# Two of three weights loaded and cast by GpSimd's queue, with a new order of all operations: sliding-window attention feeding an RWKV channel mix

## The chip, the core and the metric

The kernel runs on one core of a Trainium2 chip. The metric is the device time of one execution in microseconds; smaller is better. Before the change it is 167.43 us, the median of two runs (167.19 and 167.66). One further execution was profiled.

## What is computed

Attention over 4 batches, 8 heads, 768 positions and a head size of 64, with a window of 128 keys and 4 sink keys that every query sees. Its output, as rows of 512 features, goes into a channel mix with three weight matrices.

```python
scores = scale * np.matmul(q, k.transpose(0, 1, 3, 2))
keep = is_sink | in_window               # 4 sinks, window of 128
a = softmax(np.where(keep, scores, -1e9))
x = (a @ v) as [B, S, 512]
xk = mu_k * x + (1.0 - mu_k) * x_prev    # x_prev: x one position earlier
xr = mu_r * x + (1.0 - mu_r) * x_prev
k = np.maximum(xk @ w_k, 0.0)            # w_k 512 x 1024
v = k * k @ w_v                          # w_v 1024 x 512
r = 1.0 / (1.0 + np.exp(-(xr @ w_r)))    # w_r 512 x 512
return r * v
```

All inputs and the output are fp32; the matrix products run in bf16.

## The kernel before

**Units.** The work is cut into 12 units of 256 positions, numbered u = 0 to 11, three to a batch. For each unit the program records four groups of operations, which the functions of the same name make: `prepare` (cast q and k to bf16, transpose them on TensorE, copy the result out of PSUM, cast v), `attend` (scores, exponential, mask, product with v, division), `mix` (transpose x, form xk and xr on VectorE) and `ffn` (w_k product, ReLU and square, w_r product and tanh, w_v product, store). Units 0 and 1 get their mask as a matrix product added in PSUM (line 714), so that VectorE needn't multiply it in.

**Loads.** q, k, v and the weights come from HBM on SyncE's (SP's) queue. One unit's q or k is 512 KB and its v is two loads of 256 KB. For unit 0 the loads of q and k are halved by heads. The weights come as fp32 pieces of 1 MB (w_k in two, w_v in two, w_r in one) into three staging buffers named w32 (line 427). Ten casts then turn them into the bf16 tiles `wk_sb`, `wr_sb` and `wv_h` (lines 572 to 582): four for w_k, two for w_r and four for w_v, each of 128 x 1024 elements. On which engine each of them runs is in the table CHOICE. In the page, `wk_sb L564` on DVE and POOL and L558 on ACT are these casts.

**Order.** Nothing about the order is left to chance. The table ORDER lists for each engine (PE is TensorE, DVE VectorE, ACT ScalarE, POOL GpSimd, SP SyncE) the numbers of its operations in the order in which it issues them, and an engine that waits for one holds up all that stand behind it. A number is an operation's place in the program. `Plan.schedule` replays these lists with a cost for each operation. It does so to choose the buffer that each operation gets, and to see where TensorE would be idle: there it puts matrix products with a tile of zeros, called fills, whose result nothing reads (line 985, made in lines 264 to 275). They are there up to 32 us of planned time. How many stand at a place is fixed when the program is built. Line 241 doubles the planned cost of TensorE's operations up to 5.6 us, for a clock that isn't yet full.

**The first unit** of `ffn` can start once unit 0's xk is made (line 858) and w_k is in bf16. In the lists before the change TensorE's first w_k product, operation 206, stands behind the exponential of two head pairs of unit 1. The operations that the prediction follows there are, for units 0 and 1, the casts of line 596 (k, q) and line 644 (v), the copies out of PSUM of line 630, the exponentials of line 743 and, on POOL, the copy of the sink keys of line 661 (`ksink`).

Of the kernel before, what the change touches and what calls it, by code (L numbers as in the profile page):

```python
# [18 lines left out]
    82: "POOL", 83: "ACT", 89: "ACT", 97: "DVE", 99: "DVE", 100: "DVE", 103: "DVE", 104:  # L19
    "ACT", 137: "DVE", 140: "DVE", 141: "ACT", 143: "DVE", 150: "DVE", 178: "DVE", 181:  # L20
    "DVE", 183: "DVE", 187: "DVE", 190: "DVE", 191: "DVE", 193: "DVE", 200: "DVE", 209:
    "ACT", 213: "ACT", 217: "ACT", 258: "DVE", 270: "ACT", 271: "ACT", 276: "DVE", 292:
    "ACT", 339: "DVE", 344: "POOL", 346: "DVE", 349: "ACT", 350: "DVE", 352: "DVE", 359:
    "DVE", 367: "DVE", 372: "ACT", 376: "ACT", 380: "ACT", 419: "POOL", 421: "DVE", 422:
    "POOL", 428: "ACT", 430: "DVE", 437: "DVE", 446: "ACT", 450: "ACT", 454: "ACT", 458:
    "ACT", 497: "DVE", 499: "DVE", 500: "DVE", 505: "ACT", 527: "ACT", 535: "ACT", 576:
    "DVE", 579: "DVE", 584: "DVE", 585: "DVE", 594: "DVE", 603: "ACT", 607: "ACT", 615:
    "ACT", 654: "DVE", 660: "ACT", 661: "ACT", 663: "DVE", 679: "ACT", 683: "ACT", 691:
    "ACT", 728: "DVE", 732: "DVE", 734: "DVE", 736: "DVE", 742: "DVE", 749: "DVE", 758:
    "ACT", 762: "ACT", 766: "ACT", 770: "ACT", 807: "DVE", 811: "DVE", 813: "DVE", 814:  # L30
    "ACT", 823: "DVE", 832: "ACT", 836: "ACT", 883: "POOL", 887: "DVE", 889: "ACT", 890:
    "DVE", 892: "DVE", 899: "DVE", 907: "DVE", 908: "ACT", 916: "ACT", 920: "ACT", 958:
    "DVE", 965: "DVE", 978: "ACT", 982: "ACT", 986: "ACT", 1002: "ACT", 1013: "DVE",
# [24 lines left out]
        95, 92, 79, 108, 109, 101, 98, 118, 106, 119, 111, 115, 121, 125, 142, 132, 129,  # L58
        158, 138, 159, 149, 182, 156, 188, 135, 168, 169, 165, 234, 161, 175, 206, 171,
        207, 192, 210, 199, 211, 218, 214, 179, 215, 219, 185, 236, 297, 301, 289, 302,  # L60
        290, 298, 293, 247, 294, 239, 244, 224, 222, 250, 305, 275, 226, 255, 230, 227,
        262, 231, 282, 307, 259, 313, 268, 317, 309, 265, 310, 314, 342, 328, 365, 369,
        366, 373, 347, 374, 370, 325, 320, 395, 331, 336, 381, 351, 377, 358, 378, 383,
        406, 393, 385, 273, 420, 386, 443, 451, 444, 389, 452, 425, 390, 398, 403, 409,
        473, 414, 455, 447, 429, 448, 436, 456, 484, 471, 461, 459, 467, 498, 468, 524,
        528, 525, 529, 476, 503, 492, 552, 536, 481, 537, 487, 463, 508, 464, 517, 532,
        510, 563, 555, 533, 542, 560, 540, 577, 548, 586, 549, 600, 582, 604, 601, 605,
        566, 571, 630, 608, 612, 593, 609, 613, 616, 628, 641, 618, 544, 633, 545, 676,
        638, 677, 688, 680, 689, 681, 644, 649, 706, 662, 694, 684, 669, 620, 704, 717,
        685, 621, 692, 624, 755, 625, 756, 709, 714, 759, 720, 760, 763, 741, 764, 700,  # L70
        725, 696, 701, 739, 783, 697, 748, 767, 771, 768, 773, 786, 791, 794, 779, 775,
        780, 829, 776, 830, 837, 802, 815, 838, 833, 847, 834, 797, 845, 841, 822, 842,
        857, 859, 849, 853, 909, 905, 870, 906, 854, 850, 910, 862, 867, 917, 923, 918,
        913, 878, 891, 914, 935, 873, 921, 929, 898, 925, 933, 946, 930, 926, 971, 979,
        972, 975, 980, 976, 938, 943, 987, 949, 954, 983, 957, 984, 989, 995, 964, 991,
        996, 992, 999, 1003, 1000, 1004, 1011, 1007, 1012, 1017, 1008, 1019, 1015, 1020,
        1027, 1023, 1028, 1024,
    ),
    "DVE": (
        69, 70, 97, 100, 103, 99, 107, 80, 112, 113, 116, 117, 122, 123, 137, 126, 143,  # L80
        144, 127, 145, 181, 187, 146, 183, 140, 147, 150, 151, 148, 153, 154, 155, 152,
        81, 166, 162, 176, 163, 167, 177, 172, 173, 193, 84, 200, 194, 178, 195, 201, 196,
        202, 203, 197, 205, 198, 86, 221, 190, 238, 243, 191, 85, 204, 240, 245, 241, 249,
        246, 87, 88, 254, 276, 300, 251, 90, 256, 252, 296, 304, 257, 277, 228, 258, 232,
        278, 280, 284, 281, 339, 285, 287, 279, 288, 311, 286, 324, 346, 319, 315, 367,
        335, 330, 368, 321, 322, 326, 332, 327, 337, 333, 338, 352, 353, 359, 354, 360,
        355, 361, 362, 356, 397, 274, 421, 402, 363, 408, 357, 350, 387, 413, 399, 391,
        400, 410, 404, 405, 415, 411, 416, 364, 430, 500, 431, 437, 432, 434, 475, 438,
        497, 439, 433, 440, 491, 499, 469, 480, 486, 477, 435, 493, 478, 441, 494, 442,
        531, 482, 488, 483, 489, 509, 554, 465, 539, 559, 556, 579, 576, 512, 557, 519,  # L90
        513, 561, 562, 521, 514, 520, 515, 565, 550, 654, 570, 588, 516, 567, 572, 568,
        573, 523, 522, 594, 589, 595, 632, 584, 597, 585, 590, 637, 596, 634, 611, 635,
        591, 546, 639, 598, 640, 643, 648, 592, 599, 645, 650, 651, 663, 646, 728, 664,
        736, 665, 708, 713, 671, 672, 666, 622, 673, 667, 732, 719, 734, 626, 710, 715,
        711, 716, 724, 675, 742, 687, 721, 743, 668, 744, 726, 722, 727, 674, 702, 746,
        740, 807, 749, 790, 785, 698, 750, 811, 747, 787, 754, 745, 752, 792, 788, 751,
        793, 753, 801, 781, 777, 803, 804, 796, 817, 818, 798, 799, 819, 820, 840, 823,
        824, 826, 827, 825, 844, 887, 828, 861, 813, 866, 907, 855, 821, 851, 877, 863,
        868, 864, 869, 912, 872, 879, 892, 880, 893, 874, 875, 896, 894, 895, 899, 890,
        900, 901, 902, 942, 937, 931, 897, 927, 903, 948, 904, 953, 939, 940, 944, 945,  # L100
        974, 955, 950, 951, 958, 959, 956, 962, 960, 965, 961, 966, 967, 968, 997, 993,
        969, 970, 963, 1006, 1013, 1014, 1010, 1021, 1029, 1025,
    ),
    "ACT": (
        68, 67, 94, 91, 96, 93, 110, 114, 102, 104, 120, 124, 131, 128, 133, 130, 134,
        139, 160, 164, 157, 136, 141, 189, 174, 235, 170, 208, 83, 209, 212, 184, 180,
        216, 220, 186, 237, 242, 291, 299, 213, 303, 248, 295, 253, 223, 225, 217, 306,
# [28 lines left out]
class Plan:  # L136
# [28 lines left out]
    def schedule(self):  # L165
# [42 lines left out]
        while any(lines.values()):  # L208
            best = None
            for engine, line in lines.items():  # L210
                if not line or left[line[0]]:
                    continue
                i = line[0]
# [27 lines left out]
            if o["engine"] == "PE" and t < 5600.0:  # L241
                cost += min(cost, 5600.0 - t)
# [59 lines left out]
def kernel(  # L302
# [64 lines left out]
    def act(n):  # L367
        return 67.0 + 0.833 * n
# [669 lines left out]
```

## Time and profile before

| | us |
|---|---|
| median of the runs | 167.43 |
| time of the profiled execution | 168.37 |
| its span, first to last instruction | 166.7 |
| TensorE busy | 159.5 |
| TensorE's weight loads busy | 105.2 |
| VectorE busy | 145.6 |
| ScalarE busy | 133.6 |
| GpSimd busy | 16.3 |

The granted TensorE clock is 1.000 in the summary of the core. The span is the stretch that the profile shows; the profiled execution took 1.67 us more than it. Some rows of the page that the change touches, with the mean duration of one instruction: copies out of PSUM on ACT (line 630) 753 ns x13 and 752 ns x7, on DVE 731 ns x3 and 735 ns x1; weight casts on DVE 677 to 694 ns, on ACT 1049 and 1188 ns, on POOL 1112 ns; fp32 casts of 128 x 512 on ACT 618 to 659 ns, on DVE about 422 ns; fills (line 985) 594 ns x14.

A busy TensorE in the page isn't TensorE at its peak, since products are pipelined and their ends are modelled. The DMA line counts packets that overlap, so a stretch can show more than one full share.

### The profile page before, as it was taken

Reading aid. Unit: us, or ns where it says so; the run is one execution under the profiler, and the core shown is the slowest. Engines: PE = TensorE matmul, PEld = TensorE weight load, DVE = VectorE, ACT = ScalarE, POOL = GpSimd, SP = SyncE. Lnnn points to the kernel's source line nnn. Section 1 sums busy time; section 2 is a strip of 40 time slices with the busy share of each in tenths; the row PEclk is TensorE's granted clock in tenths of the full one; section 3 lists DMA queues with packets and bytes.
Section 4 is the critical chain, followed back from the end, with each engine's and each line's share of the span. In section 5 each row is a group of like instructions: output and inputs, shape, how many; then the busy total and the mean of one; then the engine's idle time right before and its main releaser. Section 6 shows DMA issues by size and latency. Waiting matters only on the chain.

```text
span 166.7 us, 4208 instructions
## 1 busy us (share of the span) xinstructions
PE 159.5 (96%) x1611; PEld 105.2 (63%) x1611; DVE 145.6 (87%) x378; ACT 133.6 (80%) x221; POOL 16.3 (10%) x43
## 2 busy tenths in 40 slices
PE   7999889999999999999999999999999999999991
PEld 2455567865577568486585775856575675684760
DVE  5249999999999999999999899899979988999832
ACT  3679959998999999998999999719779588754340
POOL 7800020000221201210000000210010000000000
PEclk9999999999999999999999999999999999999999
DMA  4999999999969979999996898779959782100403
GB/s 134 251 290 247 374 349 265 333 339 273 232 135 255 257 149 201 242 287 228 184 263 114 186 260 236 159 137 225 278 106 241 185 220 99 63 4 0 189 0 126
DMA packets 81762, 33.81 MB, mean 203 GB/s; under 512 B 63688, under 2 KB 76240, under 8 KB 81744
## 3 DMA queue, kind: packets, MB, share of 16 engines
q1 hardware_dynamic: 81728, 33.56, 84.7%
q8 instruction: 12, 0.20, 0.5%
q14 instruction: 6, 0.05, 0.1%
q10 hardware_dynamic: 16, 0.00, 0.0%
HBM read 24.12 MB, written 6.29 MB: 182 GB/s over the span
## 4 chain that ended last, share of the span: by engine, by line
PE 82%; DVE 8%; ACT 4%; DMA 2%; issue 2%; DVEq 0%; ACTq 0%
PE bank L908 24%; PE bank L965 22%; PE bank L947 12%; PE sc L707 6%; PE bank L781 6%; PE bank L820 3%; PE bank L622 3%; PE bank L769 2%; DMA qs<-in_q_dram 2%; ACT e L743 1%; PE bank L985 1%; PE sc L714 1%; DVE x L797 1%; PE bank L878 1%; DVE xk L858 1%
## 5 line engine op out<-in xcount | busy, mean ns | idle before, releaser
L908 PE MATMUL bank<-xk,wk_sb 128*128 128x256 bf16 x384 | 50.8, 273 | 0.8 <-DVE wk_sb L564 0.7
L743 ACT ACTIVATE e<-sc 128x1024 bf16<-128x1024 f32 (+1 forms) x48 | 45.5, 975 | 6.1 <-PE sc L707 6.0
L965 PE MATMUL bank<-wv_h,kk 128*128 128x512 bf16 x184 | 45.7, 380 | 0.0
L908 PEld LDWEIGHTS <-wk_sb 128*128 128x128 bf16 x384 | 35.5, 98 | 9.6 <-DVE wk_sb L564 1.2
L918 ACT ACTIVATE rl<-bank 128x512 bf16<-128x512 f32 x45 | 26.4, 609 | 13.9 <-PE bank L908 12.3
L965 PEld LDWEIGHTS <-kk 128*128 128x128 bf16 x184 | 16.8, 98 | 15.8 <-issue 0.5
L757 DVE TENSOR_TENSOR e<-e,mask 128x1024 bf16<-128x1024 bf16 (+1 forms) x40 | 25.2, 645 | 0.4 <-ACT e L743 0.2
L947 PE MATMUL bank<-wr_sb,xr 128*128 128x512 bf16 x96 | 24.3, 379 | 0.0
L858 DVE SCALAR_TENSOR_TENSOR xk<-td,mu_all,xt 128x256 bf16<-128x256 bf16 x48 | 22.8, 497 | 0.2
L858 DVE SCALAR_TENSOR_TENSOR xr<-td,mu_all,xt 128x256 bf16<-128x256 bf16 x48 | 22.6, 483 | 0.0
L935 ACT ACTIVATE kk<-rl 128x512 bf16<-128x512 bf16 x32 | 20.5, 646 | 0.1
L797 DVE TENSOR_TENSOR x<-bank,rec 128x256 bf16<-128x256 f32 x48 | 19.2, 415 | 0.5
L781 PE MATMUL bank<-vb,e 128*128 128x65 bf16 x352 | 18.7, 193 | 0.4 <-ACT e L743 0.3
L974 DVE SCALAR_TENSOR_TENSOR ob<-th,bank 128x512 f32<-128x512 f32 x23 | 15.6, 681 | 3.1 <-PE bank L965 2.7
L781 PEld LDWEIGHTS <-e 128*128 128x128 bf16 x352 | 16.3, 97 | 3.1 <-ACT e L743 0.9
L953 ACT ACTIVATE th<-bank 128x512 f32<-128x512 f32 x24 | 14.6, 618 | 1.9 <-PE bank L947 1.9
L707 PE MATMUL sc<-qt,kt 64*128 64x128 bf16 (+1 forms) x256 | 14.2, 242 | 0.3 <-ACT kt L630 0.3
L947 PEld LDWEIGHTS <-xr 128*128 128x128 bf16 x96 | 8.7, 98 | 7.0
L769 PE MATMUL bank<-vsink,es 128*128 128x130 bf16 x64 | 12.4, 221 | 0.1
L707 PEld LDWEIGHTS <-kt 64*128 64x128 bf16 x256 | 9.0, 95 | 5.4 <-issue 2.3
L630 ACT COPY qt<-bank 128x512 bf16<-128x512 bf16 x13 | 9.8, 753 | 1.6 <-PE bank L622 1.6
L847 DVE TENSOR_TENSOR td<-xt 128x512 bf16<-128x512 bf16 x24 | 10.6, 440 | 0.2
(75 smaller groups left out, 167.6 us busy)
## 6 DMA issues: line engine op xcount, KB each, us to landing
vs<-in_v_dram SPq DMA_DIRECT2D x24, 256.0 KB, 5.0
out_dram<-ob SPq DMA_DIRECT2D x23, 256.0 KB, 4.3
ks<-in_k_dram SPq DMA_DIRECT2D x18, 256.0 KB, 5.2
qs<-in_q_dram SPq DMA_DIRECT2D x7, 512.0 KB, 6.2
qs<-in_q_dram SPq DMA_DIRECT2D x10, 256.0 KB, 4.5
w<-in_moe_w_k_dram SPq DMA_DIRECT2D x2, 1024.0 KB, 8.3
w<-in_moe_w_v_dram SPq DMA_DIRECT2D x2, 1024.0 KB, 8.8
ks<-in_k_dram SPq DMA_DIRECT2D x3, 512.0 KB, 10.0
```

The lines of the kernel that those rows point to most:

```text
L707: nc.tensor.matmul(out=sc[:, a, o0:o1], lhsT=lhs[rows], rhs=rhs[rows], start=u not in BIAS, stop=True, skip_group_check=u in BIAS)
L743: nc.scalar.activation(out=buf[ek][:, :, lo:], in_=buf[sck][:, :, lo:], func=AF.Exp, scale=scale)
L757: nc.vector.tensor_tensor(out=at, in0=at, in1=m, op=ALU.mult)
L769: nc.tensor.matmul(out=o[:, g, :, :], lhsT=buf["es", u][:, 128 * g:128 * g + 128], rhs=vsink[b % 2][:, 2 * c:2 * c + 2, :], start=True, st ...
L781: nc.tensor.matmul(out=o[:, g, a, :], lhsT=e[:, a, e0:e0 + 128], rhs=rhs, start=(T == 0 and i == 0), stop=(i == len(blocks) - 1), skip_gro ...
L797: P.op("DVE", dve(256), lambda ok=ok, rk=rk, c=c: nc.vector.tensor_tensor(out=buf["x", u][:, :, 128 * c:128 * c + 128].rearrange("p g (a d ...
L858: nc.vector.scalar_tensor_tensor(out=buf[key][:, c0 + i, :], in0=buf[tk][:, i, :], scalar=mu[w][:, c0 + i:c0 + i + 1], in1=xt[:, c0 + i, t ...
L908: nc.tensor.matmul(out=ps[:, i, :], lhsT=wk_sb[:, c, 128 * f:128 * f + 128], rhs=xk[:, c, :], start=(c == 0), stop=(c == NC - 1), skip_gro ...
L918: nc.scalar.activation(out=buf[rk], in_=buf[psk].rearrange("p (i t) -> p i t", i=2), func=AF.Relu)
L935: nc.scalar.activation(out=buf["kk", u][:, 2 * f2:2 * f2 + 2, :], in_=buf[rk], func=AF.Square)
L947: nc.tensor.matmul(out=buf[psk], lhsT=buf["xr", u][:, c, 128 * g:128 * g + 128], rhs=wr_sb[:, c, :], start=(c == 0), stop=(c == NC - 1))
L965: nc.tensor.matmul(out=buf[psk], rhs=wv_h[:, f, :], lhsT=buf["kk", u][:, f, 128 * g:128 * g + 128], start=(f == 0), stop=(f == NF - 1))
```

## The change

**The loads of w_k and w_r.** They leave SP's queue and the staging buffers. GpSimd issues them, as a DMA that reads fp32 and writes bf16 straight into `wk_sb` and `wr_sb`. The six casts of w_k and w_r are gone, and every later operation has a number that is smaller by six. The three loads, operations 8, 9 and 12, are told to read `("v", 0, 1)`, so they wait until the second half of unit 0's v has landed. w_v is loaded and cast as it was, now from two of three staging buffers that nobody else takes.

```diff
         key = ("w32", name, i)
-        P.op("SP", 510.0, lambda: nc.sync.dma_start(out=buf[key], in_=src), rank,
-             service=2850.0, descs=660, take=[("w32", key)], writes=[(name + "32", i)])
+        if name == "wv":
+            P.op("SP", 510.0, lambda: nc.sync.dma_start(out=buf[key], in_=src), rank,
+                 service=2850.0, descs=660, take=[("w32", key)], writes=[(name + "32", i)])
+            return
+        tile = wk_sb[:, :, 512 * i:512 * i + 512] if name == "wk" else wr_sb
+        P.op("POOL", 1200.0, lambda: nc.gpsimd.dma_start(out=tile, in_=src), rank, port=True,
+             lag=1900.0, service=2850.0, descs=0, reads=[("v", 0, 1)],
+             writes=[(name, j) for j in ((2 * i, 2 * i + 1) if name == "wk" else (0, 1))])
...
     for i in range(4):
         j = i % 2
-        cast(wk_sb[:, :, 256 * i:256 * i + 256], "wk", i // 2,
-             (slice(None), slice(None), slice(256 * j, 256 * j + 256)), 2 + i, [("wk", i)])
-    for i in range(2):
-        cut = (slice(None), slice(2 * i, 2 * i + 2))
-        cast(wr_sb[cut], "wr", 0, cut, 8 + i, [("wr", i)])
```

**The fills.** A fill is 256 columns wide instead of 512, and it is put into smaller gaps of the plan. The planned cost of TensorE is doubled up to 6.2 us instead of 5.6.

```diff
-            if o["engine"] == "PE" and t < 5600.0:
-                cost += min(cost, 5600.0 - t)
+            if o["engine"] == "PE" and t < 6200.0:
+                cost += min(cost, 6200.0 - t)
...
-                while t - now > (300.0 if now > 4000.0 else 600.0) and now < self.fill_until:
+                while now < self.fill_until:
+                    one = 213.0 if now < 6200.0 else 113.0
+                    if t - now <= (0.4 * one if now < 9000.0 else one + 60.0):
+                        break
...
-                    now += 225.0 if now > 4000.0 else 430.0
+                    now += one
...
-    P.fill = lambda bank: nc.tensor.matmul(out=bank, lhsT=warm[:, 0:128], start=True,
-                                           rhs=warm.unsqueeze(1).to_broadcast([128, 2, 256]),
-                                           stop=True)
+    P.fill = lambda bank: nc.tensor.matmul(out=bank[:, 0:256], lhsT=warm[:, 0:128],
+                                           rhs=warm, start=True, stop=True)
```

**The copies of transposed q and k out of PSUM.** The two last dimensions are walked in the other order: before, the copy read PSUM in a row and wrote SBUF with a stride; now it reads PSUM with a stride and writes SBUF in a row. Some planned costs of the replay are changed with it.

```diff
                     out=buf[key][:, 2 * half:2 * half + 2, :, :].rearrange(
-                        "p c g (t j) -> p c j (g t)", j=2),
+                        "p c g (t j) -> p c (g t) j", j=2),
                     in_=buf[psk].bitcast(BF16)[:, 0:512].rearrange(
-                        "p (c j t) -> p c j t", c=2, j=2))
-            P.op("ACT", 600.0, evacuate(nc.scalar.copy), rank + half,
-                 alts={"ACT": (600.0, evacuate(nc.scalar.copy), False),
-                       "DVE": (625.0, evacuate(nc.vector.tensor_copy), False)},
+                        "p (c j t) -> p c t j", c=2, j=2))
+            P.op("ACT", 480.0, evacuate(nc.scalar.copy), rank + half,
+                 alts={"ACT": (480.0, evacuate(nc.scalar.copy), False),
+                       "DVE": (605.0, evacuate(nc.vector.tensor_copy), False)},
```

**The order.** CHOICE and ORDER are replaced as a whole. The beginnings of the lists of ACT, POOL and SP, in which the prediction reads:

```diff
     "ACT": (
-        68, 67, 94, 91, 96, 93, 110, 114, 102, 104, 120, 124, 131, 128, 133, 130, 134,
-        139, 160, 164, 157, 136, 141, 189, 174, 235, 170, 208, 83, 209, 212, 184, 180,
+        67, 68, 88, 85, 91, 90, 94, 104, 108, 96, 131, 97, 114, 98, 118, 122, 128, 124,
+        175, 158, 154, 130, 135, 151, 183, 168, 164, 229, 172, 187, 202, 194, 206, 174,
...
     "POOL": (
-        73, 71, 72, 75, 78, 76, 77, 74, 105, 82, 344, 272, 419, 422, 427, 507, 506, 737,
-        738, 883,
+        72, 73, 78, 71, 74, 76, 75, 77, 8, 9, 12, 99, 178, 411, 266, 489, 501, 500, 650,
+        732,
     "SP": (
-        1, 0, 2, 3, 4, 5, 7, 6, 16, 10, 11, 8, 9, 15, 12, 17, 18, 13, 14, 20, 19, 23, 25,
+        1, 0, 2, 3, 7, 4, 5, 6, 16, 10, 11, 15, 17, 18, 13, 14, 20, 19, 23, 25, 24, 21,
```

On SP, 0 to 3 are unit 0's k and q, 4 and 5 its v, 6 and 7 unit 1's k and q, 10 and 11 its v, 15 and 16 unit 2's k and q, 17 and 18 its v, 13 and 14 are w_v. In the new ACT list, 122 and 128 are the casts of unit 1's k, 175 the cast of a half of unit 2's q, 135 that of the second half of unit 1's v, and 158, 154, 168 and 164 are the four exponentials of unit 1. On POOL 99 is the copy of the sink keys of unit 0. In TensorE's new list the first w_k product is operation 200, behind all four products with v of unit 1 (155, 159, 169, 165).

## The prediction

> **What bounds the kernel now.** I read the page's busy times and DMA line first, then the sums by stretches of 4 us, then the chain of waits and the order of time between 4 and 24 us. The page:
>
> ```profile
> PE 159.5 (96%) x1611; PEld 105.2 (63%) x1611; DVE 145.6 (87%) x378; ACT 133.6 (80%) x221; POOL 16.3 (10%) x43
> ...
> DMA  4999999999969979999996898779959782100403
> ...
> PE 82%; DVE 8%; ACT 4%; DMA 2%; issue 2%; DVEq 0%; ACTq 0%
> ```
>
> TensorE holds 82% of the chain, and the DMA engines are full from the second slice of 4.2 us on. The stretches (PE, PEld, DVE, ACT, POOL busy, clock, DMA share, GB/s) show where TensorE isn't the limit:
>
> ```profile
> 8.00:12.00 4.00, 3.96 (x33) 1.89 (x27) 1.36 (x3) 2.72 (x4) 0.19 (x1) 1.00 1.13 281
> 12.00:16.00 4.00, 3.61 (x52) 2.32 (x46) 3.83 (x14) 3.91 (x7) 0.20 (x1) 1.00 1.28 255
> 16.00:20.00 4.00, 3.35 (x45) 1.95 (x44) 3.94 (x11) 4.00 (x7) 0.00 (x0) 1.00 1.01 343
> 20.00:24.00 4.00, 3.17 (x61) 2.40 (x58) 4.00 (x11) 2.94 (x5) 1.11 (x1) 1.00 1.10 356
> 24.00:28.00 4.00, 3.98 (x45) 3.21 (x42) 3.95 (x12) 3.38 (x6) 0.00 (x0) 1.00 1.15 322
> 28.00:32.00 4.00, 4.00 (x46) 3.31 (x44) 4.00 (x11) 4.00 (x8) 0.00 (x0) 1.00 0.91 260
> ```
>
> From 12 to 24 us DVE (11.8 of 12 us), ACT (10.9) and DMA are all full, and TensorE isn't. From 24 us to the last product at about 163 us TensorE is full. If I give each product the spacing of its kind in a dense run (215 ns for 512 columns, 109 for 256, 56 for 128, about 29 for 65), about 10 us of useful products start before 24 us and 128 after it. So the end is set by **when TensorE gets its steady supply, at 23.02 us**; a later or earlier start there moves the end one for one. What releases that start, in order of time:
>
> ```profile
> 18.00 0.41 DVE L644 CAST vb<-vs 128x512 bf16<-128x512 f32 x1
> ...
> 19.52 0.70 ACT L644 CAST vb<-vs 128x512 bf16<-128x512 f32 x1
> ...
> 20.97 1.11 POOL L564 CAST wk_sb<-w 128x1024 bf16<-128x1024 f32 x1 [8.74 <-DMA w<-in_moe_w_k_dram]
> 21.10 1.26 DVE L858 SCALAR_TENSOR_TENSOR xk<-td,mu_all,xt 128x256 bf16<-128x256 bf16 x1
> ...
> 22.28 0.68 DVE L564 CAST wk_sb<-w 128x1024 bf16<-128x1024 f32 x1
> ...
> 23.02 0.61 PE L908 MATMUL bank<-xk,wk_sb 128*128 128x256 bf16 x4 [0.74 <-DVE wk_sb L564]
> ```
>
> The first w_k product waits for a cast of w_k on DVE. The xk operation ahead took 1.26 us against a mean of 0.497, beside POOL's cast. Unit 1's v is cast at 18.0 and 19.5. Earlier, another row of the same view:
>
> ```profile
> 8.41 1.89 PE L985 MATMUL bank<-warm 128*128 128x512 bf16 x4
> ```
>
> Four fills (starts 0.42 us apart, a half clock) hold TensorE until unit 0's transposes at 10.09, though their casts were done at about 7.5.
>
> [...]
>
> **The change, part by part.**
>
> *Casts removed.* On DVE one w_k cast (0.68) ahead of 23.02 us, plus the 0.76 us (1.26 - 0.50) that POOL's cast cost its neighbour: up to 1.4 us of DVE. Later another w_k cast on DVE (0.68) and on ACT (1.05), and two of w_r on DVE (2 x 0.69): past 24 us, beside full TensorE, so nothing. w_v's casts move from 3 DVE + 1 ACT to 2 + 2; they run near 36 to 38 us, also covered.
>
> *Copies out of PSUM.* No row shows the new pattern. Bounds: no gain, or the 0.13 us that separates 753 ns from a plain ACT copy of 128x512 (about 625). I take 0.1 us each. The list has five on ACT before the last exponential of unit 1 (90, 96, 124, 130, 183): 0.5 us. The contrary, a slower strided PSUM read, I price at +0.1 us each.
>
> *Fills.* They close the idle 4.3 to 4.67 us and fill in halves, [...] and the hold to 10.09 shrinks: 1.7 us at most on TensorE. ACT gets it only as far as its new list is ready.
>
> *ACT's list replayed* with the spacings of its starts before (cast 0.51, copy 0.55, exponential 0.74 in unit 0, 1.0 in unit 1): k's cast 6.15, copy 6.7, q's cast 7.2, two exponentials 8.15 to 9.6, then 96, 131, 97, 114, 98, 118 to 13.1; 122, 128, 124, 175 to 15.2; scores and 158, 154 to 17.8; 130, 135, 151, 183 to 19.8; 168 and 164 to 21.8. All four products with v of unit 1 stand ahead of the first w_k product, so that comes at about **22.2**. That is 0.8 us earlier, and with one product with v (about 0.3 us) more behind it. It holds only if every load is there.
>
> *The loads.* This is the step that decides. Before, unit 1's k landed at 13.2 (issued 6.9, 6.3 to landing), v at 16.2 and 17.0 (9.3 + 6.9, 11.4 + 5.7), unit 2's q between, about 14.5; then w_k at 20.8 and 23.6. Unit 1's q now goes ahead of unit 0's v, so that v lands at about 9.2 + 1.7 = 10.9 (512 KB at some 300 GB/s). The weight loads wait for it and add a second full queue from about 12 us, when k, q and v above still need 17.0 - 12 = 5 us of full engines. If GpSimd's queue takes a share s of the engines' time, a load that landed at L lands at 12 + (L - 12)/(1 - s), until the weights' own 3 x 2.7 = 8.1 us are through (512 packets of 2 KB on 16 engines, 84 ns each by the packet records). The wants by the replay: k at 13.1, q of unit 2 at 14.7, v at about 18 and 18.4.
>
> - s = 0.3: k 13.7, q 15.6, v 18.0 and 19.1: ACT loses about 0.7 us; the gain is used up.
> - s = 0.5: k 14.3, q 17.0, v 20.4 and 22.0. ACT: 122 waits to 14.3, 175 to 17.0, the exponentials go to 19.5, and 135 waits to 22.0; the last exponential ends at 25.5, first w_k product about **25.7**, +2.7 us, less 0.3 for the product with v that is done.
> - s = 0.76: if queues take turns by packets, 2 KB (84 ns) against 512 B (27 ns) is 84/111: q at 22.6, v at 24.3 and 25.1; last exponential at about 29.5: +6.5 us.
>
> *POOL.* 99 (`ksink`) stands behind three DMA issues, planned at 1.2 us each; from 11 us they end at 14.6, [...]. TensorE's sink scores of unit 1 wait for it (17.19 before). Bounds 0 to 1 us; I take 0, as ACT is later by then. [...]
>
> *SP* is three issues shorter, w_v follows the same loads as before: 0. *Steady state and tail:* TensorE's list still ends in three quarter products, so no change; a stall somewhere in the new order I bound at -0.5 to +1 us.
>
> Sum for s = 0.5: +2.7 - 0.3 = +2.4, less 0.2 of what clock and copies may add: **+2.2 us** on the profiled 168.37, so 170.6. That execution is 0.94 above the median; against the median of 167.43, 169.6.
>
> **Rivals.**
> 1. *Shared DMA (forecast, 0.38):* as above, 168 to 171.5.
> 2. *The weights hide (0.32):* [...] s stays under about 0.33 and ACT's list runs as replayed: 167.43 - 1.0 = 166.4 (165.2 to 167.9). For it: v was there 1.8 and 2.5 us before its casts. Against it: the DMA line is full throughout.
> 3. *GpSimd's packets win (0.22):* s above 0.6. It decides from s = 0.33 on, and past 0.6 the loss is over 4 us: 171.5 to 176, 174 at 0.76. For it: the packet sizes. [...]
> 4. *Front relieved by more (0.08):* ACT and DVE gain 1.4 + 1.7 us and the order another: 163.5.
>
> That the casts remain isn't possible by the diff. The DMA casting slower than 84 ns a packet would be in 3.
>
> **Numbers.** Two per cent, 3.35 us, about what a measurement can tell, is 164.1 and 170.8. Faster: nearly all of rival 4, 0.07. Slower: rival 3's 0.22, the upper part of 1 (0.12) and 0.04 for a stall of the order: 0.38. The rest, 0.55, is the same. Predicted 169.6; its own range is 168 to 171.5. For 8 in 10 I take in rival 2 and half of 3: 165.3 to 174.3.
>
> **What would show it.** Right: unit 1's v and unit 2's q land 3 us or more later, casts of lines 644 and 596 wait for DMA between 14 and 22 us, w_k is there before it is wanted, the first w_k product starts near 25.7. Rival 2: no such waits, start near 22. Rival 3: start at 28 or more, with TensorE idle or filling. Wrong altogether: TensorE idle after 30 us, or copies of line 630 not near 0.65 us.

## The result, and the profile after

The changed kernel takes **175.59 us** (175.42 and 175.77), against 167.43 before: a ratio of 1.049, with an interval of 1.041 to 1.057. The profiled execution took 175.42, its span is 173.7 us, 7.0 more than before. Of the runs below, two of the four executions of e4_gate_v1, the profiled one among them, fell in a slower state of the chip; its time is the median of the other two. The rows of its page that answer to those shown of before (busy times, DMA line, chain by engine), with its clock line and the row of GpSimd's DMA queue, which isn't on the page of before:

```profile
PE 160.2 (92%) x1620; PEld 109.2 (63%) x1641; DVE 142.7 (82%) x369; ACT 135.6 (78%) x227; POOL 16.1 (9%) x43
...
PEclk9999558999999999999999999999999999999999
DMA  4999999998145999989969979759998974120303
...
q0 software_dynamic: 1584, 1.57, 5.4%
...
PE 80%; DMA 9%; SPq 4%; DVE 3%; issue 1%; ACT 1%; DVEq 0%
```

Busy times hardly moved; DMA's share of the chain went from 2% to 9%. Where that sits, the stretches show (PE, PEld, DVE, ACT, POOL busy, clock, DMA share, GB/s):

```profile
8.00:12.00 4.00, 4.00 (x43) 3.01 (x42) 2.12 (x5) 3.70 (x7) 2.16 (x5) 1.00 1.27 210
12.00:16.00 4.00, 2.40 (x33) 1.74 (x31) 2.07 (x6) 1.14 (x2) 0.00 (x0) 1.00 1.19 218
16.00:20.00 4.00, 0.17 (x2) 0.18 (x3) 0.00 (x0) 0.85 (x2) 0.00 (x0) 0.64 1.19 213
20.00:24.00 4.00, 2.56 (x27) 1.74 (x25) 1.40 (x5) 1.38 (x3) 0.00 (x0) 0.50 1.20 252
24.00:28.00 4.00, 3.83 (x27) 2.36 (x29) 3.15 (x7) 3.70 (x7) 0.61 (x1) 0.58 1.12 246
```

From 12 to 24 us VectorE is busy 3.5 us (11.8 before) and ACT 3.4 (10.9 before), while the DMA engines stay full. Their GB/s look lower than before in the stretches from 16 to 24 us (213 and 252; 343 and 356 before), but the page counts a packet that casts by the 1 KB that it writes: w_k and w_r are 3 MB of fp32, and the queue row above has 1.57 MB. Counted by what is read, it is about 355 and 283 GB/s (an estimate: GpSimd's queue wrote 0.57 and 0.12 MB in these stretches, here counted twice). So from 16 to 20 us the engines read as fast as before, but mostly weights. VectorE, ACT and TensorE wait for data. What for, the order of time says for POOL, ACT and PE:

```profile
7.31 1.62 POOL L437 DMA_DIRECT2D wk_sb<-in_moe_w_k_dram  x2
8.91 0.76 POOL L437 DMA_DIRECT2D wr_sb<-in_moe_w_r_dram  x1
...
19.15 1.14 ACT L600 CAST kb<-ks 128x512 bf16<-128x512 f32 x2 [6.01 <-DMA ks<-in_k_dram]
...
23.50 0.62 ACT L600 CAST qb<-qs 128x512 bf16<-128x512 f32 x1 [2.44 <-DMA qs<-in_q_dram]
...
30.87 0.38 PE L912 MATMUL bank<-xk,wk_sb 128*128 128x256 bf16 x2
```

Three things are to be seen. GpSimd issues its DMAs from 7.31 us, before unit 0's v is there (its first half landed at 9.76): they didn't wait for v. ACT stands still for 6.01 us until unit 1's k is there and 2.44 until unit 2's q is. The first w_k product starts at 30.87 us instead of 23.02, and from there to the last product it is 138.6 us, against 139.7 before. So the whole loss of the profiled execution is made before 31 us. The chain of waits between 8 and 32 us has one large piece, unit 2's q (start, duration, what):

```profile
8.28 15.19 DMA qs<-in_q_dram
...
23.50 0.63 ACT qb L600
...
24.17 0.62 PE bank L626 x4
...
27.36 0.77 DVE xk L862
...
30.56 0.29 PE bank L785 x4
...
31.03 0.44 PE bank L912 x4
```

What its packets stood behind, the queues show between 11 and 19 us (packets, MB, share of 16 engines in use; the records overlap):

```profile
q0 software_dynamic: 1141, 1.14, 83.5%
q1 hardware_dynamic: 1140, 0.58, 35.3%
```

The queues' packets passed in equal numbers, 1141 to 1140, and so they did in parts (568 to 567 from 12 to 16 us, 572 to 571 from 16 to 20): one for one, as in turns. GpSimd's reads 2 KB and takes 96 ns (median of the records), SP's moves 512 B in 40, so GpSimd's queue had 83.5/118.8 = 0.70 of the packets' time. Its 1536 packets are 1536 x 96 ns / 16 = 9.2 us of packet time on each engine, and they ran from 9.5 to 21.9 us. Unit 1's k landed at 19.13 us (13.16 before), unit 2's q at 23.47 (about 14.5, the prediction's estimate; the trace has no landing for it), unit 1's v at 24.54 and 25.28 (16.21 and 17.02): late by 6 to 9 us.

### The profile page after: what moved, and what is told of

Read it like the earlier page. It is cut to its first block, busy times and chain, and to the rows that moved or that the text cites. A ratio compares the mean times of both kernels' runs of the same rounds, so it can differ in the third digit from the quotient of the medians.

```text
span 173.7 us, 4241 instructions
## 1 busy us (share of the span) xinstructions
PE 160.2 (92%) x1620; PEld 109.2 (63%) x1641; DVE 142.7 (82%) x369; ACT 135.6 (78%) x227; POOL 16.1 (9%) x43
## 3 DMA queue, kind: packets, MB, share of 16 engines
q0 software_dynamic: 1584, 1.57, 5.4%
## 4 chain that ended last, share of the span: by engine, by line
PE 80%; DMA 9%; SPq 4%; DVE 3%; issue 1%; ACT 1%; DVEq 0%
PE bank L912 24%; PE bank L969 23%; PE bank L951 12%; DMA qs<-in_q_dram 9%; PE sc L711 6%; PE bank L785 6%; PE bank L824 3%; SPq L414 2%; PE bank L626 2%; PE bank L773 2%; SPq L397 2%; PE bank L882 1%; DVE xk L862 1%; PE bank L688 1%; PE bank L671 0%
## 5 line engine op out<-in xcount | busy, mean ns | idle before, releaser
L912 PE MATMUL bank<-xk,wk_sb 128*128 128x256 bf16 x384 | 50.0, 273 | 0.1
L747 ACT ACTIVATE e<-sc 128x1024 bf16<-128x1024 f32 (+1 forms) x48 | 44.1, 959 | 2.7 <-PE sc L711 2.7
L969 PE MATMUL bank<-wv_h,kk 128*128 128x512 bf16 x171 | 44.6, 379 | 0.6
L922 ACT ACTIVATE rl<-bank 128x512 bf16<-128x512 f32 x40 | 23.3, 603 | 8.6 <-PE bank L912 8.5
L939 ACT ACTIVATE kk<-rl 128x512 bf16<-128x512 bf16 x36 | 22.5, 636 | 2.4 <-DVE rl L926 2.3
L951 PE MATMUL bank<-wr_sb,xr 128*128 128x512 bf16 x88 | 23.8, 379 | 0.4
L801 DVE TENSOR_TENSOR x<-bank,rec 128x256 bf16<-128x256 f32 x48 | 19.5, 418 | 0.5
L785 PE MATMUL bank<-vb,e 128*128 128x65 bf16 x352 | 19.2, 194 | 0.0
L785 PEld LDWEIGHTS <-e 128*128 128x128 bf16 x352 | 16.8, 98 | 3.0 <-ACT e L747 0.7
L957 ACT ACTIVATE th<-bank 128x512 f32<-128x512 f32 x24 | 14.5, 604 | 4.3 <-PE bank L951 3.4
L798 DVE RECIPROCAL rec<-bank 128x4 f32<-128x4 f32 x48 | 8.0, 176 | 10.1 <-PE bank L785 8.3
L711 PE MATMUL sc<-qt,kt 64*128 64x128 bf16 (+1 forms) x256 | 14.3, 243 | 0.3 <-ACT kt L634 0.3
L851 DVE TENSOR_TENSOR td<-xt 128x512 bf16<-128x512 bf16 x24 | 10.1, 420 | 0.2
## 6 DMA issues: line engine op xcount, KB each, us to landing
ks<-in_k_dram SPq DMA_DIRECT2D x3, 512.0 KB, 12.4
```

What stands on the lines that cost most here:

```text
L711: nc.tensor.matmul(out=sc[:, a, o0:o1], lhsT=lhs[rows], rhs=rhs[rows], start=u not in BIAS, stop=True, skip_group_check=u in BIAS)
L747: nc.scalar.activation(out=buf[ek][:, :, lo:], in_=buf[sck][:, :, lo:], func=AF.Exp, scale=scale)
L785: nc.tensor.matmul(out=o[:, g, a, :], lhsT=e[:, a, e0:e0 + 128], rhs=rhs, start=(T == 0 and i == 0), stop=(i == len(blocks) - 1), skip_gro ...
L801: P.op("DVE", dve(256), lambda ok=ok, rk=rk, c=c: nc.vector.tensor_tensor(out=buf["x", u][:, :, 128 * c:128 * c + 128].rearrange("p g (a d ...
L912: nc.tensor.matmul(out=ps[:, i, :], lhsT=wk_sb[:, c, 128 * f:128 * f + 128], rhs=xk[:, c, :], start=(c == 0), stop=(c == NC - 1), skip_gro ...
L922: nc.scalar.activation(out=buf[rk], in_=buf[psk].rearrange("p (i t) -> p i t", i=2), func=AF.Relu)
```

## The experiments

**Theory 1:** the weights' packets take the engines ahead of q, k and v that are wanted sooner; the loss is the later start of the first w_k product. Rivals: the start without a wait; the new order; the half clock; a second queue by its mere use. All the kernels side by side, in us. The first two columns are of the profiled execution, from the start of the first w_k product to the start of the last product of all. The last column is the run's median, with its interval of the ratio to executions of before that were made beside it (medians of 167.4 to 167.7):

| kernel | first w_k product | to the last product | time |
|---|---|---|---|
| before | 23.02 | 139.7 | 167.43 |
| after | 30.87 | 138.6 | 175.59, 1.049 (1.041 to 1.057) |
| e1_true_gate | 28.83 | 139.6 | 174.18, 1.038 (1.033 to 1.043) |
| e3_before_pool_dma | 35.46 | 141.2 | 181.41, 1.081 (1.074 to 1.088) |
| e6_small_packets | 28.82 | 138.6 | 172.95, one run |
| e5_fills_in_stall | 30.58 | 138.8 | 175.31, 1.047 (1.041 to 1.054) |
| e2_weights_on_sp | 22.58 | 143.8 | 171.72, 1.023 (1.019 to 1.027) |
| e8_k2_ahead | 23.61 | 142.1 | 171.70, 1.024 (1.019 to 1.029) |
| e7_before_copy | 21.38 | 140.5 | 167.69, 1.001 (0.998 to 1.004) |
| e9_before_fills | 22.22 | 141.4 | 170.08, 1.013 (1.008 to 1.017) |
| e10_before_fills_copy | 21.77 | 141.4 | 169.94, 1.013 (1.008 to 1.018) |
| e4_gate_v1 | 25.35 | 145.1 | 173.80, 1.036 (1.030 to 1.041) |
| e11_gate_v1_few_fills | 24.25 | 139.2 | 170.00, 1.013 (1.009 to 1.017) |
| e12_quarter_weights | 26.47 | 138.6 | 170.40, 1.014 (1.007 to 1.020) |
| e13_quarter_vector_zeros | 23.80 | 138.6 | 168.20, 1.004 (1.002 to 1.006) |
| e14_w_k_alone | 22.88 | 139.7 | 168.22, 1.003 (1.001 to 1.004) |

**e1_true_gate: is it the missing wait?** The changed kernel, with a real wait on unit 0's v:

```diff
+        def fetch(tile=tile, src=src, first=(what == "wka")):
+            if first:
+                nc.gpsimd.tensor_copy(out=tile[0:1, 0, 0:1], in_=buf["v", 0][0:1, 1, 0, 0:1])
+            nc.gpsimd.dma_start(out=tile, in_=src)
```

> The changed kernel, with the wait on the second half of unit 0's v made real: GpSimd first copies one element of that v into the weight tile that its first load writes. In the changed kernel the three loads were issued at 7.3 to 8.9 us, before that v had landed. Theory 1 (the two queues take turns packet by packet, about 0.7 of the engines' time for GpSimd's): first weight data near 13 instead of 9.5 us, so unit 1's k lands near 13.5 instead of 19.1, but its v still only near 24 to 26 us; the first w_k product at about 30 us (30.9 in the changed kernel), time 173 to 175.5. Rival (the missing wait is the fault, and the plan with it works): v by 20 us, first w_k product by 25 us, time under 170.

It took 174.18 us. The DMAs were issued from 11.90 us and their first packet came at 14.3, 2.3 us later than the prediction had it. Unit 1's k now landed on time, at 13.15, and so did the first half of its v, but the second half only at 24.34. TensorE stood for 5.9 us up to 25.8; in the changed kernel it stood for 5.4 us up to 19.8.

```profile
25.79 0.40 PE L693 MATMUL bank<-qt,ksink 128*32 128x256 bf16 x2 [5.89 <-ACT qt L639]
```

So the missing wait is worth 1.4 of the 8.2 us; the rest comes even when the prediction's wait is there.

**e3_before_pool_dma: the loads alone.** The kernel before, its order and fills, with only w_k's and w_r's loads moved to GpSimd's queue and the six casts left out, as in the diff of the change:

```diff
-        1, 0, 2, 3, 4, 5, 7, 6, 16, 10, 11, 8, 9, 15, 12, 17, 18, 13, 14,
+        1, 0, 2, 3, 4, 5, 7, 6, 16, 10, 11, 15, 17, 18, 13, 14,
...
+        P.op("POOL", 1200.0, lambda: nc.gpsimd.dma_start(out=tile, in_=src), rank, port=True,
...
-        cast(wk_sb[:, :, 256 * i:256 * i + 256], "wk", i // 2,
```

> The kernel before with one part of the change alone: w_k and w_r loaded and cast by GpSimd's queue behind the making of the masks, their six casts left out; old order, old fills, old copies. Theory 1: the loads alone do it, first w_k product near 30 us, time 173 to 177. Rival (the new order made the kernel sensitive): under 170.

181.41 us, more than expected. Unit 1's k landed at 21.23, and TensorE waited for it:

```profile
21.93 0.61 PE L624 MATMUL bank<-ident,kb 128*128 128x128 bf16 x4 [8.86 <-ACT kb L598]
```

The first w_k product came 12.4 us later than before. Part of that are fills: 22 in a row, from 26.6 to 31.5 us, stood ahead of TensorE's sink scores, and ACT stood idle for 4.6 us until these were made. Without these 4.6 us, 7.8 are left, as in the changed kernel (7.9), with none of its other parts; that the two add up like this is an estimate.

**e6_small_packets: the size of a packet.** The changed kernel with each weight load in four of 128 columns:

```diff
-        P.op("POOL", 1200.0, lambda: nc.gpsimd.dma_start(out=tile, in_=src), rank, port=True,
+        def fetch(tile=tile, src=src):
+            for j in range(4):
+                cols = slice(128 * j, 128 * j + 128)
+                nc.gpsimd.dma_start(out=tile[:, :, cols], in_=src[:, :, cols])
```

> The changed kernel with each 1 MB weight load of GpSimd's queue cut into four of 128 columns, so that a packet reads 512 B instead of 2 KB; the bytes are the same. Theory 1 (the queues take turns packet by packet, so the size of GpSimd's packets sets its share): share near a half; unit 1's k lands near 17 instead of 19.1 and unit 2's q near 20 instead of 23.5, while the weights come later, the second half of w_k near 30 and w_r near 38 us or later. What the time does is open, since w_k is then late. Rival (the engines' time is shared by bytes or evenly): landings as in the changed kernel within 0.7 us.

The queues between 11 and 19 us:

```profile
q0 software_dynamic: 2371, 0.59, 74.7%
q1 hardware_dynamic: 2477, 1.15, 63.5%
```

The numbers are nearly equal again (2371 to 2477), now with nearly equal packets: a share of 74.7/138.2 = 0.54. Microsecond by microsecond they differ before 18 us (103 to 516 from 12 to 13 us), while GpSimd is still issuing its twelve loads; from 18 to 23 us it is 1720 to 1672. In e1, too, the first two microseconds (15 to 17) have 355 to 120, and the next six 945 to 942. SP's queue moved 1.15 MB instead of 0.58, unit 1's k landed at 15.85 instead of 19.13, unit 2's q at about 19.0 instead of 23.47, and the first w_k product came 2.1 us earlier, with the same bytes loaded. So in these two runs the packet's size set the share: 0.70 with 2 KB, 0.54 with 512 B. What binds is now the second half of unit 1's v, which came no sooner than in the changed kernel (25.15 and 25.28):

```profile
25.18 0.62 ACT L653 CAST vb<-vs 128x512 bf16<-128x512 f32 x1 [3.18 <-DMA vs<-in_v_dram]
```

The small packets cost more in sum: 6144 of 40 ns are 15.4 us on 16 engines, against 9.2. So the 2.1 us aren't the whole worth of an even share, and the time rests on one execution.

**e5_fills_in_stall: the half clock.** 46 zero products more before unit 1's k is transposed, ahead of the stretches in which the granted clock was 0.50 to 0.64 (16 to 28 us):

```diff
+                if (u, name, half) == (1, "k", 0):
+                    for _ in range(46):
+                        P.fill(buf[psk])
```

> The changed kernel with 46 more fills (about 5 us at full clock) ahead of the transposes of unit 1's first k half, where TensorE stood idle for 5.4 us and its clock went down to half until 28 us. Theory 1 (the loss is the late load of unit 2's q, and the chain from it to the first w_k product is mostly DVE and ACT): clock full between 16 and 24 us, but the first w_k product earlier by no more than 1 us; time 174 to 176. Rival (the half clock is half of the loss): first w_k product before 28.5 us, time under 173.

The mean clock rose from 0.971 to 0.986, and the time stayed (175.31). In the changed kernel products of 512 columns started 427 ns apart from 26.3 us on, at a granted clock of 0.50, and 216 ns apart from 13.2 us on, at 1.00. With the added products the clock was full from 16 to 20 us (0.64 in the changed kernel), from 20 to 28 us it was 0.76 and 0.81 (0.50 and 0.58). So only a part of the half clock was taken away, and the first w_k product came 0.3 us earlier: the half clock lies mostly where TensorE waits anyway.

**e2_weights_on_sp and e8_k2_ahead: the new order without GpSimd's DMAs.** e2 is the changed kernel with w_k and w_r back on SP's queue and their six casts back in their places in the lists (numbered 1025 to 1030). In e8 unit 2's k goes ahead of w_k as well. The lists of SP, after to e2 and e2 to e8:

```diff
-        1, 0, 2, 3, 7, 4, 5, 6, 16, 10, 11, 15, 17, 18, 13, 14,
+        1, 0, 2, 3, 7, 4, 5, 6, 16, 10, 11, 8, 9, 15, 12, 17, 18, 13, 14,
...
-        1, 0, 2, 3, 7, 4, 5, 6, 16, 10, 11, 8, 9, 15, 12, 17, 18, 13, 14,
+        1, 0, 2, 3, 7, 4, 5, 6, 16, 10, 11, 15, 8, 9, 12, 17, 18, 13, 14,
```

> The changed kernel with w_k and w_r loaded by SP's queue into staging buffers and cast on DVE, ACT and POOL as before the change, at the places in the lists that these loads and casts had before; everything else (fills, copies, new order) stays changed. Theory 1: the whole loss of 8 us is the loads, so the first w_k product comes at 22 to 24 us and the time is 166 to 169. Rival (the new order or the fills cost something of their own): over 170.

> The run with the weights back on SP's queue (171.7 us), with one load moved: unit 2's k goes ahead of both halves of w_k instead of behind them. There it landed at 25.9 us and ACT waited 3.7 us for it, with copies for TensorE behind. Theory 1 (that wait is what was left of the loss; the new order has no cost of its own): k lands near 21, w_k near 23 and 25.5, time 167 to 169. Rival (the new order is worse in itself): over 170.

Both miss what theory 1 expected, at 171.7 us; the number given for the rival, over 170, is met. In e2 the first w_k product does come at 22.58, as replayed (22.2), but then ACT's list stands for unit 2's k:

```profile
25.90 0.62 ACT L595 CAST kb<-ks 128x512 bf16<-128x512 f32 x1 [3.72 <-DMA ks<-in_k_dram]
```

In e8 that wait is gone, and the next one is a cast of w_k on VectorE, which holds up all behind it in its list, and later one of w_r in front of TensorE:

```profile
22.46 0.69 DVE L570 CAST wk_sb<-w 128x1024 bf16<-128x1024 f32 x1 [1.29 <-DMA w<-in_moe_w_k_dram]
...
35.84 1.02 PE L946 MATMUL bank<-wr_sb,xr 128*128 128x512 bf16 x3 [1.14 <-DVE wr_sb L570]
```

So with the old loads the new order is slower than the old one, and what it waits for are a load (e2) and casts (e8). These two runs don't show what it costs in itself: both also keep the finer fills, which cost 1.3% alone (e9, below). That it isn't the loss of the changed kernel, e13 shows.

**e7, e9, e10: the small parts alone.** The kernel before with the new copies (e7), with the finer fills (e9), with both (e10). The diffs are the change's own, of the copies and of the fills:

```diff
-                        "p c g (t j) -> p c j (g t)", j=2),
+                        "p c g (t j) -> p c (g t) j", j=2),
...
-                    now += 225.0 if now > 4000.0 else 430.0
+                    now += one
```

> The kernel before with the new form of the copy of transposed q and k out of PSUM alone (PSUM read with a stride, SBUF written in a row). Copies on ACT took 0.75 us before and 0.58 to 0.60 in the changed kernel, on DVE 0.73 and 0.69. Theory 1: seven of these copies lie on ACT before the first w_k product, which is set by DVE and by w_k's landing too; first w_k product 0 to 0.8 us earlier, time 0 to 1 us less. Rival (the copies matter nowhere): no change within 0.3 us.

> The kernel before with the finer fills alone (half-width zero products, put into smaller gaps, and the start-up doubling to 6.2 us). Loads, casts, copies and order are those of before. Theory 1 (the loss of the changed kernel lies in its DMA traffic ahead of 31 us, and the fills are worth next to nothing because ACT and the loads, not TensorE, set the start of the first w_k product): first w_k product between 22.3 and 23.1 us, time within 0.6 us of before, so 166.8 to 168. Rival A (a clock that is full 3 us earlier is a gain that the changed kernel hid): 164.5 to 166.5. Rival B (fills push useful products back): over 168.5.

> The kernel before with both small parts of the change, finer fills and the copies in the other order, and its own loads, casts and order. Theory 1: the same as with fills alone or up to 0.5 us less, 166.3 to 167.8, since ACT has five shorter copies of about 0.17 us before the last exponential of unit 1. Rival: the two together bring 1.5 us or more (under 165.9), which would make this the version to keep.

In e7 the copies became 0.16 us shorter on ACT (590 and 596 ns against 753 and 752) and 0.05 on VectorE. The first w_k product came 1.6 us earlier than in the profile of before, and the time stayed. The finer fills made it 1.3% longer, beyond what theory 1 expected, though the first w_k product came 0.8 us earlier; e10 is as slow. In e9 TensorE waits later:

```profile
40.24 0.40 PE L625 MATMUL bank<-ident,qb 128*128 128x128 bf16 x4 [0.63 <-ACT qb L599]
...
138.14 0.62 PE L710 MATMUL sc<-qt,kt 64*128 64x256 bf16 x12 [0.51 <-DMA qt<-qb]
```

The first is unit 3's q, which landed at 39.55 (38.21 before); SP had issued the w_v load ahead of it 1.2 us later. The profile shows these two waits, 1.1 of some 2.2 us; that the fills cause them by way of the plan's buffers wasn't tried. Of the two gains foreseen at the front neither reached the end.

**e4_gate_v1 and e11_gate_v1_few_fills: the weights behind unit 1's v.** e4 puts them behind a real wait on the first half of unit 1's v, with the sink keys' copy ahead on GpSimd. e11 is e4 with the planned fills ended at 22 us instead of 32.

```diff
-LOADS = ("kq0", "v0", "kq1", "wka", "wkb", "v1", "wr", "wva", "wvb")
+LOADS = ("kq0", "v0", "kq1", "v1", "wka", "wkb", "wr", "wva", "wvb")
...
+                nc.gpsimd.tensor_copy(out=tile[0:1, 0, 0:1], in_=buf["v", 1][0:1, 0, 0, 0:1])
...
-    P.fill_until = 32000.0
+    P.fill_until = 22000.0
```

> The changed kernel with the three weight loads made to wait for the first half of unit 1's v (a real wait, by a copy of one element), and the sink-key copy moved ahead of them on GpSimd. Theory 1: k, q and v land as early as before (13, 14.5, 16 to 17 us), ACT's list runs as I replayed it, and the weights come from about 18.4 us at 0.7 of the engines: w_k at 23 and 27, w_r at 31 us. First w_k product near 23.5, a second wait for the other half of w_k near 27; time 167 to 170. Rival [...]: w_k's first half after 27 us, time over 172.

> The kernel e4_gate_v1 (weights by GpSimd's queue behind a real wait on unit 1's v) with the plan's fills ended at 22 us of planned time instead of 32, so that the fills which stood in front of TensorE at 28 to 36 us are gone. Theory 1 (late weights, not the queue they come by, are what is left): w_k lands near 25 and 28.6 us as in e4, first w_k product 24.8 to 25.5, then at its pace, so 169 to 171.5. Rival (the fills cost nothing, what stalled TensorE there was the wait for weights or for ACT and DVE, whose work comes late in this order): 172.5 to 175.5, with TensorE idle where the fills were.

e4 took 173.8 us, more than theory 1 gave. Unit 1's k and v and unit 2's q were on time, w_k landed at 25.2 and 28.6 and the first w_k product came at 25.35, but 42 fills, 4.75 us from 29.2 on, then stood in TensorE's list, and ACT waited 4.4 us for what stood behind them. With the fills ended earlier it is 170.0, inside what theory 1 gave. What is left are waits for w_k itself:

```profile
24.25 0.60 PE L917 MATMUL bank<-xk,wk_sb 128*128 128x256 bf16 x4 [1.07 <-DMA wk_sb<-in_moe_w_k_dram]
```

**e12 and e13: the packets taken away.** Each weight load fetches a quarter of its rows, and the rest of `wk_sb` and `wr_sb` is set to zero, by GpSimd in e12 and by VectorE in an idle time in e13. In both, three quarters of the sums of the w_k and w_r products are left out; every product is still made. e12's edit, and what e13 has in place of its first line:

```diff
+            nc.gpsimd.memset(tile[:, 1:4, :], 0.0)
+            nc.gpsimd.dma_start(out=tile[:, 0, :], in_=src[:, 0, :])
...
+                    nc.vector.memset(wk_sb[:, 1:4, :], 0.0)
+                    nc.vector.memset(wr_sb[:, 1:4, :], 0.0)
```

> The changed kernel in which each of GpSimd's three weight loads fetches only a quarter of its rows (128 packets of 2 KB in place of 512); the other three quarters of w_k and w_r are set to zero by GpSimd, so the output leaves out three quarters of the w_k and w_r products' sums while every product is still made. Everything else is the changed kernel's. Theory 1 (the loss is the DMA time of the weights ahead of q, k and v, about 3/4 of 9 us, and the new order is good if its loads are there): unit 1's k lands at 13.5 to 15.5, unit 2's q before 18, first w_k product at 22 to 25 us, time 166 to 169. Rival A (the new order is slow in itself, by TensorE, ACT or DVE, whatever the loads): first w_k product at 22 to 25 as well, but 170.5 to 173. Rival B [...]: first w_k product at 28 or later, over 173.

> As e12_quarter_weights (each of GpSimd's weight loads fetches a quarter of its rows, the rest of w_k and w_r is zero, so three quarters of their sums are left out), but VectorE writes the zeros, in its idle time at 3.4 to 6.2 us. Theory 1 (the packets are the loss; the rest of e12 was its zeroing): no cast of VectorE near 3 us, unit 2's q there before 17, first w_k product at 22.5 to 24.5 us, last product 138.6 us later as in the changed kernel, so 166.3 to 168.5. Rival A (the order itself starts w_k late): first w_k product still after 25.5, time over 169. Rival B (a second queue costs by being there, not by its bytes): the loads of q, k and v land as late as in the changed kernel, over 172.

e12 came out between the theories, because the zeroing cost something of its own. One VectorE cast lasted 3.05 us beside GpSimd's memsets, where the same cast takes 0.42 in e13:

```profile
9.75 3.05 DVE L604 CAST qb<-qs 128x512 bf16<-128x512 f32 x1
```

Without that, e13 starts the first w_k product 7.1 us earlier than the changed kernel and takes 168.20:

```profile
23.80 0.60 PE L924 MATMUL bank<-xk,wk_sb 128*128 128x256 bf16 x4
```

The order, the fills, the copies and the queue are the changed kernel's, and from the first w_k product on it takes the same 138.6 us. 1152 of 1536 packets, 6.9 us of packet time, are gone, and with them 7.4 of the 8.2 us. GpSimd still issues three DMAs from 7.3 us on, with a quarter of the packets, so the mere use of a second queue costs little: the run is 0.4% (0.2 to 0.6) over the kernel before.

**e14_w_k_alone: the bytes in another order.** e11, with unit 2's v and what follows it on SP held until w_k is there:

```diff
+                        if held:
+                            nc.gpsimd.tensor_copy(out=buf[key][0:1, 0, 0, 0:1],
+                                                  in_=wk_sb[0:1, 0, 512:513])
```

> As e11_gate_v1_few_fills, with unit 2's v and all that follows it on SyncE's queue (w_v, unit 3's k and q) held until w_k's second half has landed, by a one-element copy on GpSimd. Theory 1 (w_k was late because it shared the engines): w_k lands near 22 and 24.8 us in place of 24.1 and 27.5, first w_k product at 23.0 to 23.5 (then its xk and the products with v bind), time 168.4 to 169.6. Rival A (what is held comes too late: unit 2's v, w_v or unit 3's q and k make TensorE wait after 30 us): 170 to 173. Rival B (it wasn't the sharing): w_k lands no earlier, time as e11, 169.8 to 170.5.

w_k landed at 22.75 and 25.29 (24.11 and 27.47 in e11), the first w_k product came at 22.88, and the time is 168.22, 0.2 below what was expected. No wait for w_k is left; the next is for unit 3's q, which was held as well:

```profile
40.86 0.38 PE L637 MATMUL bank<-ident,qb 128*128 128x128 bf16 x4 [0.70 <-DVE xt L844]
```

In this view the wait carries VectorE's name; unit 3's q had landed only at 40.0 us, and the chain of waits runs through it. This is the changed kernel's idea with its loads in order: 7.4 us better than the change, and 0.3% (0.1 to 0.4) over the kernel before. No kernel beat that one.

## Why the prediction was wrong, point by point

**What bounds the end was right.** In the changed kernel the start of TensorE's steady supply set the end almost one for one: 30.87 - 23.02 = 7.85 us at the start, 7.05 in the two profiled executions and 8.16 between the medians. "Steady state" was bounded at -0.5 to +1 us and came to -1.1 (138.6 against 139.7 us). It isn't a rule, though: e7 and e9 start 1.6 and 0.8 us earlier than before and are no faster, and e2 starts 0.4 us earlier and takes 4 us more. The start sets the end only where nothing waits after it.

**The step that failed is the loads**: the share of s = 0.5 and the time from which it counts. The forecast said that "the weight loads wait for it [v] and add a second full queue from about 12 us", and chose an even share. Measured: first packet at 9.5 us, share 0.70. With an even share from 9.5 us the forecast's own formula gives unit 2's q at 19.5 us and v's second half at 24.5, in place of 17.0 and 22.0. e6 is near that case (0.54 from 9.4 us) and has about 19.0 and 25.15. So the early start alone accounts for 2.5 of the 5.2 us between the 25.7 us forecast for the first w_k product and the 30.87 measured. Mending one of the two isn't enough: with the wait made real (e1) and with the share brought to 0.54 (e6) the first w_k product comes at 28.8 us both times, not at 25.7. No run has both, and which weighs more isn't shown; without most of the packets (e13) the loss is gone.

The prediction's own row for s = 0.76 gave unit 2's q at 22.6 us, unit 1's v at 24.3 and 25.1, and +6.5 us. Measured are 23.47, 24.54 and 25.28, and +7.85. That row came with a chance of 0.22. Turns by packets stand in it as an assumption of the author's: 81728 of the 81762 packets of before were on one queue, so that profile couldn't show it. It was worked out, but not believed; with packets of 84 and 27 ns, as they are in that profile, turns can't give even shares. The changed kernel's trace agrees with turns, at 1141 to 1140 packets, and GpSimd needed only 2.4 us for all three issues.

**The wait that isn't there.** That operations 8, 9 and 12 are told to read v orders only the plan, so what the section on the change says, that they wait until it has landed, isn't true on the chip. The DMA touches no byte of v, and it was issued at 7.31 us, 2.4 us before v's first half landed. In e1, where an element of v is copied into the DMA's tile, that copy waited 4.03 us for v, and the DMA was issued at 11.90. This could have been seen before the run: `load_weight` names no tile of v in what it issues.

**The start's arithmetic.** The row for 0.76 comes down to a simpler sum, an estimate too, which doesn't ask when the weights start: a load that is mostly behind them comes late by their whole time. The row has 8.1 us for it (84 ns a packet), measured are 9.2 (96 ns). Unit 2's q (about 14.5 to 23.47) and unit 1's v (16.21 to 24.54) were 9.0 and 8.3 late. That 9.2 fits so well is in part luck. Packet records overlap: alone, in e14, 1000 of these packets passed in 5 us, so that all 1536 would take 7.7 at that rate, an estimate. And SP's own packets took longer beside them, 40 ns against 33 between 11 and 19 us before.

**ACT's list.** The replay was right: 21.8 us for the end of unit 1's exponentials and 22.2 for the first w_k product, and 21.9 and 22.58 measured in e2, whose loads up to there were on time. It named unit 1's k, unit 2's q and v's second half as what ACT would wait for; the first two waits came, and v landed before ACT reached it. In e1 and e6 ACT waits for v's second half.

**The casts removed** were put at up to 1.4 us of VectorE. No run measures this gain alone. With the casts back, the new order loses 4.1 (e2) and 2.4 us (e8) after its first w_k product; of the waits shown for it, two in e8 are for casts, 1.29 and 1.14 us.

**Copies**: 0.1 us each was taken, 0.16 came on ACT; e7 shows no change of the time, so pricing them at nearly nothing was right. **Fills**: up to 1.7 us at the front were allowed, 0.8 came in e9, and the run was 1.3% longer, some 2.2 us; no such loss was foreseen. In the changed kernel itself, 138.6 us from the first w_k product on leave no sign of it. There TensorE did come to its full rate sooner: before, products of 128 columns started 107 ns apart up to 10.3 us and 56 from there on; after, those of 384 columns started 320 ns apart up to 6.6 us and 163 from 6.9 on.

**POOL**: taken as 0, between 0 and 1 us. The copy of the sink keys ran at 9.64, long before anyone waited. The small share of rival 2 (under about 0.33), an estimate of the author's, wasn't seen: it was 0.70, with three issues of 0.75 to 0.88 us and 2.2 us from the first issue to the first packet. VectorE was only half busy then (2.1 of 4 us from 8 to 12 us); what becomes of such issues beside a full VectorE isn't shown.

**Rival 3 came about**, for the reason given for it, the packet sizes (2 KB against 512 B). Its signs (start at 28 or later, TensorE idle) are those of the page.

## What to carry to other kernels

Bytes that are wanted later mustn't share the DMA engines with bytes that are wanted sooner, whatever queue they come by (7.4 of the 8.2 us here, by e13): in these traces a second queue added no bandwidth while the engines were full (about 355 GB/s read from 16 to 20 us, against 343 before), and its packets passed one for one with the first's (1141 to 1140), so the queue of the larger packets had more of the engines' time (0.70 with 2 KB against 512 B). When a load is moved, list what every load behind it is wanted for and when, and count the moved load's engine time against those. A dependence that only the plan knew was no wait on the chip (issue at 7.31 us, v from 9.76 on), and one copied element made it one (issue at 11.90, in e1): look for bytes that both operations touch, or for the wait itself in the trace.

## What was not expected of the hardware

- GpSimd's queue took 2.2 to 2.4 us from the start of a DMA's issue to its first packet (7.31 to 9.52 us after the change, 11.90 to 14.3 in e1), and between 1.6 (e14) and 3.4 us (e12) elsewhere. The issue itself is up to 0.88 us of that; counted from its end it was 1.3 and 1.5 us after the change and in e1. The forecast had left 1.1 us in all, from v at 10.9 us to the second queue at 12.
- A casting packet that reads 2 KB and writes 1 KB took 96 to 98 ns, also when little else ran (e14), against 84 for a plain packet of 2 KB in the kernel before. By rate they are near each other: alone, in e14, 200 casting packets passed per us, and 189 plain ones in e1 between 29 and 32 us. So casting on the way, with half the bytes to write, saved next to no DMA time.
- Beside two of GpSimd's memsets in SBUF (1.4 us each, in e12) a VectorE cast took 3.05 us instead of 0.42, and ended 0.3 us after the second of them. In the profile of before the xk operation beside GpSimd's cast (1.11 us) had taken 1.26 us, 0.76 over its mean.
